# Two weight blocks by plain products instead of a seven-product scheme, in a fused attention, gated layer and expert layer kernel

## The chip, the cores and the metric

One core of one Trainium2 chip runs the whole program. The metric is the time of one execution on the device in microseconds (us). Shorter is better. The kernel before takes 825.68 us, the median of 3 runs (825.63 to 825.71).

## The reference

Three layers follow each other, in float32.

```python
# attention: 4 sequences, 8 heads, 576 positions, head size 64
scores = scale * q @ k.T ; scores + bias where 0 <= rel < 128, else -1e9
attn = softmax(scores) ; x = attn @ v          # 2304 tokens x 512
# gated layer, 512 -> 1536 -> 512
gate = 1 / (1 + exp(-(x @ w_gate))) ; val = x @ w_val
x = (gate * val) @ w_out
# expert layer: 8 experts, one per token by the largest cosine logit
h = maximum(x[mask] @ w1[e], 0) ; out[mask] = gate_w * (h @ w2[e])
```

The change touches the attention's last units and the products `x @ w_gate` and `x @ w_val`.

## The kernel before

**Attention** runs in 36 units (`unit_s`, `unit_n`, `unit_t`, `unit_b`). A unit is 256 query positions of two heads. TensorE (PE) makes its scores (24 small matmuls, L220, tile `s`), VectorE (DVE) adds the bias and takes the maximum in four "tails" (L231), ScalarE (ACT) takes the exponential (L234), DVE makes the reciprocal sums `rs` (L249, L250), GpSimd (POOL) scales the rows (L111), PE transposes them (L263, tile `t`), the transposes are copied to `tt` by ACT (L99) and DVE (L101), and PE multiplies them by v (L285, L291), again in `t`. The results are copied into `xf`, one tile per group of tokens ("chunk") and half of the 512 features. In a loop step i stand the transposes of unit i, the product with v of unit i-1 and the scores of unit i+3. A unit's scores take both buffers `s`, so they wait for the tails of the unit before.

**The gated layer's first products** go by 12 blocks of 128 columns of w_gate and w_val (index f). A float32 number is split into a high part and a rest (`split_x` for x, `split_w` for weights, each a cast on ACT, L99, and a 128x1024 subtraction on DVE, L115), and a product of two such pairs takes three matmuls (`product`, L403), so a piece of 256 features is six matmuls of 128x512. A raw block is loaded as two tiles `wr` (`load_w`), and made from 64-bit words by `conv_w` (one ACT operation and three on DVE, L125 to L128, for each half).

**The scheme.** Four chunks of 512 tokens form two pairs. For a pair, a block of weights and the x of two chunks are a 2x2 by 2x2 product, and `seven` makes it with seven products (`m1` to `m7`) instead of eight, from A11, A12, A22 and B11, B21, B22 as they are, and from sums of x, S1 to S4 (`sum_x`, one 128x1024 DVE operation each, L313, then split), and of weights, T1 to T4 (`sum_w`, four DVE operations L365 to L369, then split). `rg` and `rv` are the products of a chunk left over (12 matmuls of 128x256 each, L460).

The weights and their sums are also stored to device memory (`wf_d`, `tf_d`) and loaded again by `load_wt` for the second pair, where only the splits are left to do.

**The order** is written by hand. In units 0 to 19 the table `AT` (L515) lists for a loop step the work of the gated layer that stands behind it. From unit 20 on ("mixed units") a list `todo` holds the pieces, and beside each the work that is recorded with it; `run(n)` takes the next n. `STEPS` gives 3, 4 and then 5 pieces to a unit, 77 in all; the other pieces follow after the last unit. For all but the first blocks the work is that of `bulk(f)`, the preparation of block f+1. In units 10 to 19 only PE and POOL keep the written order, and a scheduler orders DVE and ACT; in the mixed units all four keep it. Every engine works its list in order, so an instruction that waits holds those behind it. All tiles of x and weights come from one pool of 33 buffers.

**The start.** `load_qk` and `load_v` bring a unit's q, k and v; `cst` brings the distance table `relm` and a tile `cs` with the identity for the transposes.

Of the kernel before, what the change touches and what calls it, by code (L numbers as in the profile page):

```python
# [27 lines left out]
P = 128  # L28
# [29 lines left out]
def attn_ffn_moe(ctx: ExitStack, tc: tile.TileContext, qkd, vd, wgv, w_out, emb, tau, w1, w2, cst, ids, out):  # L58
# [257 lines left out]
    def builds(pair):  # L316
        one, two = PAIRS[pair]

        def src(half, k):
            return xf[PAIRS[pair][half], k]  # L320

        return {
            "S1+": lambda: sum_x((pair, "S1"), src(1, 0), src(1, 1), ALU.add),
            "S3+": lambda: sum_x((pair, "S3"), src(1, 0), src(0, 0), ALU.subtract),
            "S2+": lambda: sum_x((pair, "S2"), xf[pair, "S1"], src(0, 0), ALU.subtract),
            "S4+": lambda: sum_x((pair, "S4"), src(0, 1), xf[pair, "S2"], ALU.subtract),
            "A11": lambda p="hl": split_x((pair, "A11"), src(0, 0), p),
            "A12": lambda p="hl": split_x((pair, "A12"), src(0, 1), p),
            "A22": lambda p="hl": split_x((pair, "A22"), src(1, 1), p),
            "S1": lambda p="hl": split_x((pair, "S1"), xf[pair, "S1"], p),  # L330
            "S2": lambda p="hl": split_x((pair, "S2"), xf[pair, "S2"], p),
            "S3": lambda p="hl": split_x((pair, "S3"), xf[pair, "S3"], p),
            "S4": lambda p="hl": split_x((pair, "S4"), xf[pair, "S4"], p),
        }
# [22 lines left out]

    def sum_w(f, part="01"):
        if f < KF:
# [46 lines left out]
    def gate_out(f, gate, val, t0, n):  # L406
        nc.vector.scalar_tensor_tensor(out=gate, in0=gate, scalar=1.0, in1=val, op0=ALU.add, op1=ALU.mult)
        nc.sync.dma_start(gT_d[f * P:(f + 1) * P, t0:t0 + n], gate)

    def seven(pair, f, banks, rest):  # L410
# [58 lines left out]

        def piece(mm, ev):  # L470
            def both():
                mm()
                ev()

            both.mm, both.ev = mm, ev
            return both

        out = {
# [14 lines left out]
    nc.sync.dma_start(relm[:, 0:4 * P], cst[:, 0:4 * P])  # L493
    load_qk(1)
    load_v(0)
    nc.sync.dma_start(cs, cst[:, 8 * P:])
    load_qk(2)
    load_v(1)
# [10 lines left out]
    def latest(*engines):  # L509
# [6 lines left out]
        5: [lambda: split_x("rest", xf[0, 0], "h")], 6: [lambda: split_x("rest", xf.pop((0, 0)), "l")],  # L516
        12: [bA["S1+"]], 13: [bA["A22"], lambda: load_w(0)], 14: [bA["S1"], lambda: conv_w(0, 0)],
        15: [lambda: conv_w(0, 1), lambda: load_w(1)], 16: [lambda: sum_w(0)],
        17: [bA["A11"], lambda: split_w(0, 0, 0)], 18: [bA["S3+"], lambda: split_w(0, 0, 1)],
        19: [bA["S3"], bA["S2+"], sA[0]["rg"]], 20: [bA["S2"], sA[0]["rv"]],  # L520
    }
    AB = {}
    with tc.manual_schedule(engines={ENG.PE, ENG.DVE, ENG.Activation, ENG.Pool}):
# [16 lines left out]
        unit_n(0)  # L540
        tails = unit_s(2, True)
        keep_warm(3)
        load_qk(6)
        unit_t(0)
        for t in tails:
            t()
        unit_n(1)
        for i in range(SPLIT):
# [45 lines left out]

    for f in range(KF):
        names, work = "m1 m2 m5 m6 rg m7 rv m4 m3", bulk(f)
        if f == 0:
            names = "m1 m5 m6 m7 m2 m4 m3"
            work = {
                0: [lambda: load_w(2), lambda: bA["A12"]("h")],  # L600
                1: [lambda: bA["A12"]("l"), lambda: conv_w(1, 0, "a")],
                2: [bA["S4+"], lambda: conv_w(1, 1, "a")],
                3: [lambda: bA["S4"]("h"), lambda: conv_w(1, 0, "b")],
                4: [lambda: bA["S4"]("l"), lambda: conv_w(1, 1, "b")],
                5: [lambda: split_w(0, 1, 0, "h"), lambda: sum_w(1)],
                6: [lambda: split_w(0, 1, 0, "l")],
            }
        elif f == 1:
            work[0].insert(0, lambda: split_w(0, 1, 1, "h"))
            work[1].insert(0, lambda: split_w(0, 1, 1, "l"))  # L610
        todo += [(sA[f][n], work.get(z, [])) for z, n in enumerate(names.split())]
# [86 lines left out]
    for t in ("A11", "A12", "S1+", "S1", "S2+"):  # L698
        run(1)
        bB[t]()  # L700
    split_w(1, 0, 0)
    run(2)
# [11 lines left out]
    for f in range(KF):  # L714
        s, t = sv[f], sv[f + 1] if f + 1 < KF else None
        s["m5"]()
        if f == 0:
            bB["A22"]()
            bB["S4+"]()
        split_w(1, f + 1, 0)  # L720
        s["m6"]()
# [522 lines left out]
```

## Time and profile before

| | |
|---|---|
| runs | 825.63 to 825.71 us, median 825.68 |
| the profiled execution | 824.9 us, of which the span from first to last instruction is 823.1 |
| PE, weight loads of PE, DVE, ACT, POOL busy | 97%, 80%, 67%, 54%, 21% of the span |
| granted TensorE clock | 0.996 of full speed, mean |

The share of a whole span hides stages. The kernel has one of attention alone (to about 47 us), one of attention with the preparation of the first block (to about 78), the mixed units, the second pair, and then the output product and the experts. The section with the rows has busy times by stretch. In a timeline a row's bracket is the idle time of that engine ahead of the instruction, and what ended it.

### The profile page before, as it was taken

Reading aid. Unit: us, or ns where it says so; the run is one execution under the profiler, and the core shown is the slowest. Engines: PE = TensorE matmul, PEld = TensorE weight load, DVE = VectorE, ACT = ScalarE, POOL = GpSimd, SP = SyncE. Lnnn points to the kernel's source line nnn. Section 1 sums busy time; section 2 is a strip of 40 time slices with the busy share of each in tenths; the row PEclk is TensorE's granted clock in tenths of the full one; section 3 lists DMA queues with packets and bytes.
Section 4 is the critical chain, followed back from the end, with each engine's and each line's share of the span. In section 5 each row is a group of like instructions: output and inputs, shape, how many; then the busy total and the mean of one; then the engine's idle time right before and its main releaser. Section 6 shows DMA issues by size and latency. Waiting matters only on the chain. (4 is left out here: it accounts for less than half of the span.)

```text
span 823.1 us, 15426 instructions
## 1 busy us (share of the span) xinstructions
PE 794.6 (97%) x5586; PEld 656.0 (80%) x5587; DVE 548.5 (67%) x1386; ACT 446.7 (54%) x942; POOL 174.6 (21%) x263
## 2 busy tenths in 40 slices
PE   8989799999999999999999999999999999999996
PEld 5767577888888788887777777778788988978885
DVE  6999887877788888788555544547645545545443
ACT  6888666766555666658455554435334434434331
POOL 5877332322100000000010000131322030230110
PEclk9999999999999999999999999999999999999999
DMA  8685655745555486668144555251565544453510
GB/s 268 191 257 177 223 194 194 238 156 179 174 186 208 158 276 230 220 227 257 56 128 145 144 141 156 82 138 55 183 228 171 190 170 141 151 203 118 175 69 19
DMA packets 67568, 141.45 MB, mean 172 GB/s; under 512 B 8440, under 2 KB 28664, under 8 KB 67490
## 3 DMA queue, kind: packets, MB, share of 16 engines
q1 hardware_dynamic: 63586, 130.32, 48.8%
q0 software_dynamic: 3904, 10.12, 3.7%
q8 instruction: 45, 0.74, 0.4%
q14 instruction: 33, 0.27, 0.1%
HBM read 104.14 MB, written 36.93 MB: 171 GB/s over the span
## 5 line engine op out<-in xcount | busy, mean ns | idle before, releaser
L806 PE MATMUL y<-wo,gh 128*128 128x512 f32 x432 | 139.3, 397 | 0.0
L986 PE MATMUL h<-xe,weh 128*128 128x256 f32 (+4 forms) x512 | 106.3, 301 | 0.9 <-DVE h L989 0.8
L111 POOL TENSOR_SCALAR p<-p,rs 128x192 f32<-128x192 f32 x140 | 80.3, 590 | 103.5 <-DVE rs L250 57.7
L1002 PE MATMUL z<-weh,h 128*128 128x512 f32 (+3 forms) x320 | 102.0, 396 | 0.0
L806 PEld LDWEIGHTS y<-wo,gh 128*128 128x128 f32 x432 | 79.9, 188 | 18.4 <-issue 3.3
L115 DVE TENSOR_TENSOR wel<-wer,weh 128x1024 fp32r<-128x1024 f32 x64 | 78.1, 1223 | 19.1 <-ACT weh L99 18.2
L986 PEld LDWEIGHTS h<-xe,weh 128*128 128x128 f32 x512 | 83.7, 189 | 3.3 <-DVE h L989 1.9
L806 PE MATMUL y<-wo,gl 128*128 128x512 f32 x216 | 84.9, 394 | 0.0
L988 ACT ACTIVATE h<-h 128x256 fp32r<-128x256 f32 (+4 forms) x64 | 26.6, 417 | 96.8 <-PE h L986 92.4
L234 ACT ACTIVATE p<-p,mx 128x192 f32<-128x192 f32 x144 | 64.0, 447 | 24.7 <-DVE mx L231 23.9
L986 PE MATMUL h<-xe,wel 128*128 128x256 f32 (+4 forms) x256 | 76.4, 300 | 0.2 <-DVE wel L115 0.2
L99 ACT CAST weh<-wer 128x1024 fp32r<-128x1024 f32 x64 | 66.2, 1048 | 7.0 <-DMA wer<-in_w 7.0
L1002 PEld LDWEIGHTS z<-weh,h 128*128 128x128 f32 (+3 forms) x320 | 56.7, 180 | 14.0
L1002 PE MATMUL z<-wel,h 128*128 128x512 f32 (+3 forms) x160 | 62.7, 392 | 0.0
L1007 POOL DMA_INDIRECT out<-y,cols x19 | 24.4, 1284 | 171.6 <-DVE y L1006 154.8
L989 DVE SCALAR_TENSOR_TENSOR h<-h,h 128x256 fp32r<-128x256 f32 (+4 forms) x64 | 29.6, 464 | 38.4 <-ACT h L988 35.5
L1006 DVE TENSOR_SCALAR y<-z,xg 128x512 f32<-128x512 f32 (+3 forms) x22 | 16.5, 749 | 56.0 <-PE z L1002 49.1
L900 POOL DMA_INDIRECT tab_d<-ids_sb,ai x18 | 18.3, 1015 | 158.7 <-DVE ai L897 136.5
L822 ACT ACTIVATE xr<-y 128x512 f32<-128x512 f32 x18 | 10.8, 598 | 73.4 <-PE y L806 66.3
L986 PEld LDWEIGHTS h<-xe,wel 128*128 128x128 f32 x256 | 48.4, 190 | 0.7 <-DVE wel L115 0.6
L806 PEld LDWEIGHTS y<-wo,gl 128*128 128x128 f32 x216 | 40.6, 188 | 8.0
L827 DVE COPY xT<-tl 128x512 f32<-128x512 f32 x18 | 12.4, 692 | 40.6 <-PE tl L826 40.6
(332 smaller groups left out, 1933.1 us busy)
## 6 DMA issues: line engine op xcount, KB each, us to landing
wer<-in_w SPq DMA_DIRECT2D x64, 512.0 KB, 4.3
gl<-gT_d SPq DMA_DIRECT2D x27, 512.0 KB, 5.6
wr<-in_wgv SPq DMA_DIRECT2D x24, 512.0 KB, 4.9
gT_d<-c SPq DMA_DIRECT2D x48, 256.0 KB, 2.0
qk<-in_qkd SPq DMA_DIRECT2D x36, 320.0 KB, 3.3
v<-in_vd SPq DMA_DIRECT2D x36, 192.0 KB, 4.0
wf_d<-wf SPq DMA_DIRECT2D x12, 512.0 KB, 2.9
tf_d<-tf SPq DMA_DIRECT2D x12, 512.0 KB, 3.4
```

Of the source, the lines that this page charges most:

```text
L99: nc.scalar.copy(o, i)
L111: nc.gpsimd.tensor_scalar(out=t, in0=t, scalar1=r, scalar2=0.0, op0=ALU.mult, op1=ALU.add)
L115: e.tensor_tensor(out=o, in0=i, in1=h.bitcast(F32), op=ALU.subtract)
L234: nc.scalar.activation(out=o, in_=o, func=AF.Exp, scale=-1.0, bias=mx[:, z:z + 1], accum_out=su[:, z:z + 1])
L806: nc.tensor.matmul(m, g[:, k % 4, u * P:(u + 1) * P], w[:, k % 3, :], start=(k == 0 and z == 0), stop=(k == KF - 1 and z == 2))
L900: nc.gpsimd.indirect_dma_start(out=tab_d, out_offset=IOA(ap=ai[:, u:u + 1], axis=0), in_=ids_sb[:, t:t + 1], in_offset=None)
L986: nc.tensor.matmul(m[:, :n], w[:, fs], x[:, k, :], start=(cnt == 0), stop=(cnt == 3 * KD - 1))
L988: nc.scalar.activation(out=hh, in_=m[:, :n], func=AF.Relu)
L989: nc.vector.scalar_tensor_tensor(out=hl, in0=m[:, :n], scalar=0.0, in1=hh.bitcast(F32), op0=ALU.max, op1=ALU.subtract)
L1002: nc.tensor.matmul(m[0:w, :], h, ww[:, ds], start=(cnt == 0), stop=(cnt == 3 * KE - 1))
L1006: nc.vector.tensor_scalar_mul(y[0:w, :], m[0:w, :], x[0:w, DM:DM + 1])
L1007: nc.gpsimd.indirect_dma_start(out=out, out_offset=IOA(ap=idx[0:w], axis=0), in_=y[0:w, :], in_offset=None, bounds_check=NT - 1, oob_is_er ...
```

## The change

Blocks 0 and 1 of the first pair are made by a new function `eight`, which takes eight plain products; they need no S and no T, but a split of A21. The blocks from 2 on keep the scheme. The S sums and their splits, which stood in `AT` and beside block 0, now stand beside the pieces of blocks 0 and 1. The T sums of blocks 0 and 1 are made at the start of the second pair, from the weights that are loaded again (`store=False`), so their two stores and two loads fall away. `rg` and `rv` of block 0 stand one step earlier. The list of pieces has 108 entries, where it had 106. At the start, q and k of the third unit are loaded third, v of the first unit after `cs`, and the third unit's tails are no longer put behind the first unit's transposes.

```diff
+NC = 2
...
+            "A21": lambda p="hl": split_x((pair, "A21"), src(1, 0), p),
...
-    def sum_w(f, part="01"):
+    def sum_w(f, part="01", store=True):
...
-                nc.sync.dma_start(tf_d[f * P:(f + 1) * P, :], flat(t))
+                if store:
+                    nc.sync.dma_start(tf_d[f * P:(f + 1) * P, :], flat(t))
...
-            for z, (d, src) in enumerate(((wf, wf_d), (tf, tf_d))):
+            for z, (d, src) in list(enumerate(((wf, wf_d), (tf, tf_d))))[:1 if f < NC else 2]:
...
+    def eight(pair, f):
+        st = {}
+
+        def mm(kind, chunk, half):
+            k = kind, chunk
+            if half == 0:
+                st[k] = pt("m", f"{kind}{pair}{chunk}_{f}", 3)
+            product(st[k], wq[pair, f, f"B{half + 1}{1 if kind == 'g' else 2}"], xs[pair, f"A{chunk}{half + 1}"], half == 0)
+
+        def ev(kind, chunk):
+            if kind == "g":
+                st["t", chunk] = row(f"th{pair}{chunk}_{f}")[:, 0:512]
+                nc.scalar.activation(out=st["t", chunk], in_=st["g", chunk], func=AF.Tanh, scale=0.5)
+            else:
+                gate_out(f, st["t", chunk], st["v", chunk], tok(PAIRS[pair][chunk - 1]), 512)
...
     load_qk(1)
+    load_qk(2)
+    nc.sync.dma_start(cs, cst[:, 8 * P:])
     load_v(0)
-    nc.sync.dma_start(cs, cst[:, 8 * P:])
-    load_qk(2)
...
-        12: [bA["S1+"]], 13: [bA["A22"], lambda: load_w(0)], 14: [bA["S1"], lambda: conv_w(0, 0)],
-        15: [lambda: conv_w(0, 1), lambda: load_w(1)], 16: [lambda: sum_w(0)],
-        17: [bA["A11"], lambda: split_w(0, 0, 0)], 18: [bA["S3+"], lambda: split_w(0, 0, 1)],
-        19: [bA["S3"], bA["S2+"], sA[0]["rg"]], 20: [bA["S2"], sA[0]["rv"]],
+        12: [bA["A21"]], 13: [bA["A22"], lambda: load_w(0)], 14: [lambda: conv_w(0, 0)],
+        15: [lambda: conv_w(0, 1), lambda: load_w(1)], 16: [lambda: split_w(0, 0, 0)],
+        17: [bA["A11"]], 18: [sA[0]["rg"], bA["S1+"]], 19: [sA[0]["rv"]], 20: [lambda: conv_w(1, 0)],
...
-        tails = unit_s(2, True)
+        unit_s(2)
         keep_warm(3)
         load_qk(6)
+        unit_n(1)
         unit_t(0)
-        for t in tails:
-            t()
-        unit_n(1)
...
+        (cA[0]["g2a"], [lambda: load_w(2), lambda: bA["A12"]("h")]),
+        (cA[0]["g2b"], [lambda: bA["A12"]("l"), lambda: conv_w(1, 1, "a")]),
+        (cA[0]["v2a"], [lambda: conv_w(1, 1, "b"), lambda: split_w(0, 1, 0, "h")]),
+        (cA[0]["v2b"], [lambda: split_w(0, 1, 0, "l"), lambda: bA["S1"]("h")]),
+        (cA[0]["g1a"], [lambda: bA["S1"]("l")]),
+        (cA[0]["g1b"], [bA["S3+"]]),
+        (cA[0]["v1a"], [bA["S2+"], lambda: bA["S3"]("h")]),
+        (cA[0]["v1b"], [lambda: bA["S3"]("l")]),
+        (sA[1]["rg"], [bA["S4+"], lambda: bA["S2"]("h")]),
+        (cA[1]["g2a"], [lambda: bA["S2"]("l"), lambda: conv_w(2, 0, "a"), lambda: load_w(3)]),
+        (cA[1]["g2b"], [lambda: conv_w(2, 0, "b"), lambda: conv_w(2, 1, "a")]),
+        (sA[1]["rv"], [lambda: conv_w(2, 1, "b"), lambda: split_w(0, 2, 0, "h")]),
+        (cA[1]["v2a"], [lambda: sum_w(2, "0")]),
+        (cA[1]["v2b"], [lambda: sum_w(2, "1"), lambda: bA["S4"]("h")]),
+        (cA[1]["g1a"], [lambda: split_w(0, 2, 0, "l")]),
+        (cA[1]["g1b"], [lambda: bA["S4"]("l"), lambda: split_w(0, 2, 1, "h")]),
+        (cA[1]["v1a"], [lambda: split_w(0, 2, 1, "l")]),
+        (cA[1]["v1b"], []),
...
+    sum_w(0, store=False)
     split_w(1, 0, 0)
...
+        if f + 1 < NC:
+            sum_w(f + 1, store=False)
         split_w(1, f + 1, 0)
```

On DVE at the start, ahead of unit 3's tails (`p0`, `p1`, `p2` are the rows of units 0 to 2, `tt0` the copies of unit 0's transposes), the order before is:

```order
L109 TENSOR_SCALAR p0_154<-p0_154,rs0_199 128x192 x2
L101 COPY tt0_0_229<-t0_0_228 128x384
L101 COPY tt0_1_235<-t0_1_234 128x384
L231 ISA p2_220,mx2_221<-s2_0_206,edge2_0_132 128x192
...
L249 TENSOR_SCALAR rs1_248<-su1_183 128x4
L250 RECIPROCAL rs1_248<-rs1_248 128x4
L109 TENSOR_SCALAR p1_181<-p1_181,rs1_248 128x192 x2
```

and with the change:

```order
L110 TENSOR_SCALAR p0_154<-p0_154,rs0_199 128x192 x2
L232 ISA p2_220,mx2_221<-s2_0_206,edge2_0_132 128x192
...
L250 TENSOR_SCALAR rs1_236<-su1_183 128x4
L251 RECIPROCAL rs1_236<-rs1_236 128x4
L110 TENSOR_SCALAR p1_181<-p1_181,rs1_236 128x192 x2
L102 COPY tt0_0_244<-t0_0_243 128x384
L102 COPY tt0_1_250<-t0_1_249 128x384
```

Unit 2's tails and the scaling of `p1` moved ahead of the copies of unit 0's transposes.

On DVE at steps 15 to 17, with the first block's preparation (`xl` is the rest of a split x, `wl00_0` the rest of block 0's weights, `tf0` its T sums, `tt15` and `tt17` copies of transposes), before:

```order
L115 TENSOR_TENSOR xl_(0, 'S1')_1215<-xq_(0, 'S1')_1076,xh_(0, 'S1')_1214 128x1024
L101 COPY xf2_0_1102<-t14_1_1155 128x128
L249 TENSOR_SCALAR rs17_1251<-su17_1203 128x4
L101 COPY tt15_1_1230<-t15_1_1229 128x384
...
L365 TENSOR_TENSOR tf0_1359<-wf0_1218 128x256
L366 TENSOR_TENSOR tf0_1359<-wf0_1218 128x256
L368 TENSOR_TENSOR tf0_1359<-wf0_1218,tf0_1359 128x256
L101 COPY tt17_1_1372<-t17_1_1371 128x384
L369 TENSOR_TENSOR tf0_1359<-wf0_1218,tf0_1359 128x256
```

and with the change:

```order
L102 COPY tt15_1_1228<-t15_1_1227 128x384
L102 COPY xf2_0_1104<-t14_1_1157 128x128
L250 TENSOR_SCALAR rs17_1249<-su17_1205 128x4
L251 RECIPROCAL rs17_1249<-rs17_1249 128x4
...
L116 TENSOR_TENSOR wl00_0_1358<-wf0_1216,wh00_0_1357 128x1024
L102 COPY tt17_1_1368<-t17_1_1367 128x384
L102 COPY xf2_2_1385<-t16_1_1298 128x128
```

The split of S1 and the four operations of the T sums are gone from here, and the split of block 0's weights, which stood behind A11's, has their place.

On DVE around the first mixed units, before, ahead of the first piece's need for S2 (`sg0_0` is the output of block 0's `rv`):

```order
L115 TENSOR_TENSOR xl_(0, 'S3')_1570<-xq_(0, 'S3')_1501,xh_(0, 'S3')_1569 128x1024
L313 TENSOR_TENSOR xq_(0, 'S2')_1573<-xq_(0, 'S1')_1076,xf2_0_1102 128x1024
L101 COPY xf2_2_1389<-t19_1_1513 128x128
L407 SCALAR_TENSOR_TENSOR sg0_0_1588<-sg0_0_1588,r_0_1575 128x256
L249 TENSOR_SCALAR rs22_1643<-su22_1558 128x4
L250 RECIPROCAL rs22_1643<-rs22_1643 128x4
L115 TENSOR_TENSOR xl_(0, 'S2')_1607<-xq_(0, 'S2')_1573,xh_(0, 'S2')_1606 128x1024
```

and with the change, where these sums stand now, beside the outputs `th02_0` and `th01_0` of block 0's `v2` and `v1`:

```order
L116 TENSOR_TENSOR wl00_1_1713<-wf1_1602,wh00_1_1712 128x1024
L410 SCALAR_TENSOR_TENSOR th02_0_1695<-th02_0_1695,v02_0_1701 128x512
L116 TENSOR_TENSOR xl_(0, 'S1')_1742<-xq_(0, 'S1')_1508,xh_(0, 'S1')_1741 128x1024
...
L314 TENSOR_TENSOR xq_(0, 'S2')_1814<-xq_(0, 'S1')_1508,xf2_0_1104 128x1024
...
L116 TENSOR_TENSOR xl_(0, 'S3')_1817<-xq_(0, 'S3')_1799,xh_(0, 'S3')_1816 128x1024
L410 SCALAR_TENSOR_TENSOR th01_0_1801<-th01_0_1801,v01_0_1807 128x512
L314 TENSOR_TENSOR xq_(0, 'S4')_1863<-xf2_2_1385,xq_(0, 'S2')_1814 128x1024
```

S1's and S3's splits and the sums S2 and S4 moved behind the split of block 1's weights and between the outputs of block 0.

## Rows read from the trace of the kernel before

**Rows 1.** The page's part 1: busy time of each engine, its share of the span.

```profile
PE 794.6 (97%) x5586; PEld 656.0 (80%) x5587; DVE 548.5 (67%) x1386; ACT 446.7 (54%) x942; POOL 174.6 (21%) x263
```

**Rows 2.** Busy time of each engine in five stretches, granted clock, DMA share, GB/s.

```profile
20.00:47.00 27.00, 25.61 (x538) 21.32 (x533) 24.15 (x127) 23.20 (x92) 22.20 (x56) 1.00 0.66 191
47.00:78.00 31.00, 26.20 (x430) 20.29 (x428) 29.55 (x112) 25.93 (x87) 22.26 (x41) 0.94 0.76 243
78.00:116.00 38.00, 32.59 (x321) 25.78 (x320) 31.90 (x77) 25.80 (x68) 15.99 (x22) 1.00 0.56 190
116.00:220.00 104.00, 101.70 (x941) 84.62 (x940) 81.71 (x205) 68.11 (x181) 28.17 (x46) 1.00 0.59 193
255.00:290.00 35.00, 34.44 (x167) 28.53 (x167) 31.25 (x35) 21.86 (x31) 0.00 (x0) 1.00 0.52 177
```

**Rows 3.** Timeline of DVE, first 14 us: start, us, instruction, idle before it.

```profile
7.19 0.41 DVE L795 CAST tri<-cs 128x128 bf16<-128x128 f32 x1 [0.52 <-DMA cs<-in_cst]
...
10.44 1.02 DVE L101 COPY tt<-t 128x384 f32<-128x384 f32 x2 [0.74 <-PE t L263]
```

**Rows 4.** Timeline of PE: the start, and units 18 to 20 to the first product.

```profile
12.11 1.39 PE L220 MATMUL s<-qk 64*64 64x128 f32 x24 [1.30 <-issue]
...
68.43 1.30 PE L220 MATMUL s<-qk 64*64 64x128 f32 x24
69.66 0.87 PE L263 MATMUL t<-cs,p 128*128 128x128 f32 x6
70.47 0.66 PE L285 MATMUL t<-tt,v 128*64 128x128 f32 x8
...
72.19 0.43 PE L220 MATMUL s<-qk 64*64 64x128 f32 x2
...
73.73 0.39 PE L460 MATMUL r<-xh_rest,wh 128*128 128x256 f32 x1
...
78.11 0.48 PE L403 MATMUL a<-xh_(0, 'A11')_1428,wh 128*128 128x512 f32 x1
```

**Rows 5.** Timeline of DVE, 55 to 72 us.

```profile
55.07 1.36 DVE L115 TENSOR_TENSOR xl_(0, 'S1')_1215<-xq_(0, 'S1')_1076,xh_(0, 'S1')_1214 128x1024 fp32r<-128x1024 f32 x1
...
63.57 0.56 DVE L365 TENSOR_TENSOR tf<-wf 128x256 f32<-128x256 f32 x1
64.05 0.41 DVE L366 TENSOR_TENSOR tf<-wf 128x256 f32<-128x256 f32 x1
...
67.11 1.37 DVE L115 TENSOR_TENSOR xl_(0, 'A11')_1429<-xf,xh_(0, 'A11')_1428 128x1024 fp32r<-128x1024 f32 x1
...
69.22 1.23 DVE L115 TENSOR_TENSOR wl<-wf,wh 128x1024 fp32r<-128x1024 f32 x1
...
71.60 1.36 DVE L313 TENSOR_TENSOR xq_(0, 'S3')_1501<-xf,xf 128x1024 f32<-128x1024 f32 x1
```

**Rows 6.** Timeline of PE, 86 to 142 us: the waits of blocks 0 and 1, and later.

```profile
86.09 0.50 PE L403 MATMUL a<-xh_(0, 'S3')_1569,wh 128*128 128x512 f32 x1 [1.09 <-ACT r L437]
...
95.62 0.50 PE L403 MATMUL a<-xh_(0, 'A11')_1428,wh 128*128 128x512 f32 x1 [1.04 <-ACT wh L99]
...
98.54 0.50 PE L403 MATMUL a<-xh_(0, 'A11')_1428,wl 128*128 128x512 f32 x1 [2.18 <-DVE wl L115]
...
108.86 0.50 PE L403 MATMUL a<-xh_(0, 'S3')_1569,wh 128*128 128x512 f32 x1 [1.08 <-ACT r L437]
...
116.36 0.39 PE L403 MATMUL a<-xh_(0, 'A11')_1428,wh 128*128 128x512 f32 x1
...
141.59 1.03 PE L285 MATMUL t<-tt,v 128*64 128x128 f32 x8 [0.77 <-ACT tt L99]
```

**Rows 7.** Timeline of PE: the first of six matmuls of two products in a row.

```profile
221.02 0.40 PE L403 MATMUL a<-xh_(0, 'A11')_1428,wh 128*128 128x512 f32 x1
...
222.40 0.39 PE L403 MATMUL b<-xh_(0, 'A12')_1661,wh 128*128 128x512 f32 x1
```

More of the change, by code (lines that the diff above doesn't have):

```diff
@@ L408, in gate_out, with piece, both @@
         nc.sync.dma_start(gT_d[f * P:(f + 1) * P, t0:t0 + n], gate)
+    def piece(mm, ev):
+        def both():
+            mm()
+            ev()
+        both.mm, both.ev = mm, ev
+        return both
+    def eight(pair, f):
[11 more added lines that the diff above has]
+                gate_out(f, st["t", chunk], st["v", chunk], tok(PAIRS[pair][chunk - 1]), 512)
+        out = {}
+        for kind in "gv":
+            for chunk in (1, 2):
+                out[f"{kind}{chunk}a"] = piece(lambda k=kind, c=chunk: mm(k, c, 0), lambda: None)
+                out[f"{kind}{chunk}b"] = piece(lambda k=kind, c=chunk: mm(k, c, 1), lambda k=kind, c=chunk: ev(k, c))
+        return out
     def seven(pair, f, banks, rest):
@@ L468, in rest_ev @@
                 gate_out(f, st["sg"][:, 0:256], m, tok(0), 256)
[L470 to L476, printed above, removed]
         out = {
@@ L516, in attn_ffn_moe @@
         5: [lambda: split_x("rest", xf[0, 0], "h")], 6: [lambda: split_x("rest", xf.pop((0, 0)), "l")],
-        12: [bA["S1+"]], 13: [bA["A22"], lambda: load_w(0)], 14: [bA["S1"], lambda: conv_w(0, 0)],
-        15: [lambda: conv_w(0, 1), lambda: load_w(1)], 16: [lambda: sum_w(0)],
-        17: [bA["A11"], lambda: split_w(0, 0, 0)], 18: [bA["S3+"], lambda: split_w(0, 0, 1)],
-        19: [bA["S3"], bA["S2+"], sA[0]["rg"]], 20: [bA["S2"], sA[0]["rv"]],
+        12: [bA["A21"]], 13: [bA["A22"], lambda: load_w(0)], 14: [lambda: conv_w(0, 0)],
+        15: [lambda: conv_w(0, 1), lambda: load_w(1)], 16: [lambda: split_w(0, 0, 0)],
+        17: [bA["A11"]], 18: [sA[0]["rg"], bA["S1+"]], 19: [sA[0]["rv"]], 20: [lambda: conv_w(1, 0)],
     }
+    cA = [eight(0, f) for f in range(NC)]
     AB = {}
@@ L593, in bulk @@
         }
-    for f in range(KF):
-        names, work = "m1 m2 m5 m6 rg m7 rv m4 m3", bulk(f)
[L597 to L610, printed above, removed]
+    todo += [(p, w) for p, w in [
+        (cA[0]["g2a"], [lambda: load_w(2), lambda: bA["A12"]("h")]),
[16 more added lines that the diff above has]
+        (cA[1]["v1b"], []),
+    ]]
+    for f in range(NC, KF):
+        names, work = "m1 m2 m5 m6 rg m7 rv m4 m3", bulk(f)
+        if f == NC:
+            work[0] = [lambda: load_w(4), lambda: conv_w(3, 0, "a")]
         todo += [(sA[f][n], work.get(z, [])) for z, n in enumerate(names.split())]
```

## The prediction

> **What bounds the kernel now.** I read the busy shares first. PE is busy 97% of the span [rows 1], so in most of the kernel only fewer matmuls would help, and this change adds some. The second view, busy time by stretch, tells where that is not so [rows 2]. From 116 to 220 us PE works 101.70 of 104. From 47 to 78 us it works 26.20 of 31, and there DVE is full: 29.55 of 31. From 78 to 116 us PE works 32.59 of 38, with DVE at 31.90. So PE loses 4.8 and 5.4 us in these two stretches, and about 2.3 in the next 104 us. The third view is the timeline of PE. From 78 to 116 us four waits make up all of the 5.4: 1.09 and 1.08 for an ACT copy that frees a bank, and 1.04 and 2.18 at the first product of block 1, for the high part and the rest of that block's weights [rows 6]. From 47 to 78 us the waits are short and many; there the timeline of DVE shows no gaps, only attention's tails with 128x1024 operations between them [rows 5].
>
> Behind 116 us PE is the bound, so whatever lets it get there earlier or later counts in full.
>
> **What is added to PE.** Two blocks take eight products instead of seven. Where PE runs without a wait, the first matmuls of two products in a row stand 1.38 us apart [rows 7]. Two products more: +2.76 us. The two entries more in the list of pieces are these products, nothing else. The plain products also spare block 0 and block 1 three ACT copies and three DVE additions each; these are beside PE's work, and I count them only as room.
>
> **Before the first product.** I follow DVE, since it is full there.
>
> At the start, DVE idles 0.74 us for unit 0's transposes and then copies them, with unit 2's tails behind [rows 3]; scores of unit 3 wait 1.30 us for those tails' buffers [rows 4]. With the tails ahead of the copies the 0.74 is filled. But `cs` now lands behind a 320 KB tile instead of a 192 KB one, and DVE already waits 0.52 us for it with unit 1's tails queued behind [rows 3]. Bounds: a loss as large as that wait, 0.5, and a gain of the whole 1.30. I take a gain of 0.4, nearer to the 0.74 that DVE can fill than to the wait of PE, because from there on DVE's next tails follow on without a gap.
>
> Up to the tails of unit 20, which end where the split of A11 begins at 67.11 [rows 5], DVE loses S1's split (1.36) and the four T operations (0.56 and 0.41, twice: 1.94); S1's sum and A21's split are one 128x1024 operation each and cancel. It gains, ahead of these tails, block 0's weight split (1.23), which stood behind them. Net 1.36 + 1.94 - 1.23 = 2.07. With the 0.4 of the start these tails end at 67.11 - 2.47 = 64.64, and then the scores of unit 21 can start.
>
> From there on PE has more to do than DVE. Its path to the first product: scores of unit 21 (0.9, an estimate under the 1.30 that they took at 68.43, since the stretch's granted clock of 0.94 is a mean over a slow part and a full one), transposes of 19 (0.81, from 69.66 to 70.47), unit 18 with v (1.2, from 70.47 to 72.19 less a wait), and then scores of 22, `rg`, unit 19 with v, `rv` and transposes of 20, which took from 72.19 to 78.11, or 5.92 [rows 2, 4]. That is 8.83, and the first product starts at 73.47 instead of 78.11: **-4.64 us**, the start included. Bounds: if DVE's freed time came back only as its sum after the start, 2.07; if PE recovered all that it idles before 78 us in this stretch, 4.8 + 1.3 = 6.1. `rg` one step earlier costs nothing, since PE has room in front of it.
>
> **From the first product to block 2.** Before, block 2 starts at 116.36 [rows 6]. The four waits sum to 5.39. I expect them to go. The two for the ACT copy belong to m6 and m7, which use one bank; `eight` has no such pair, and its three banks let a product start while two others are read out. The two for block 1's weights came since their split was queued on DVE behind block 0's S and T work. Now it stands ahead of S1's split, and block 1's first product is the tenth piece where it was the eighth.
>
> What is late next is block 2's split. DVE was busy 31.90 us between block 0's first product and block 2's [rows 2]. It loses the T sums of block 1 (1.94), their split (1.23) and six additions of outputs there, and gets S1's and S3's splits and S3's sum (1.36 or 1.37 each [rows 5]); some 32 us or less. PE has 32.59 + 2.76 = 35.35 for the same pieces and units, and DVE can begin while PE is still on its 5.92 us from unit 22's scores to the first product: 41 together. DVE idled 38 - 31.90 = 6.1 us in that stretch before; 32 + 6.1 fits under 41. So I leave no wait there, but little room. One wait I do add: the mixed units' transposes are both copied by ACT, and unit 20's copies stand behind four exponentials while only one piece covers them. The nearest row is such a wait later, 0.77 [rows 6]; bounds 0 and 2.18, the longest wait of this stretch. Sum of this part: -5.39 + 2.76 + 0.77 = **-1.86 us**.
>
> **Behind it.** Blocks 2 to 8 keep their pieces and work. The waits of 116 to 220 us (2.3) fall where a block's start meets a unit's; the two pieces more shift this, I count no change.
>
> At the start of the second pair DVE gets two more sums, eight 128x256 operations of 0.41 to 0.56: +3.9 us at most. In 255 to 290 us it is busy 31.25 of 35, so 3.75 is free, and PE idles 0.56 there [rows 2]. Bounds: 0, and 3.9 if none of the free time lies where it helps. I take +0.2: the scheduler put other operations into DVE's gaps. The two stores and two loads of 512 KB that fall away hide beside PE now, and are worth nothing. SP's queue gets shorter; the weight loads in it come no later.
>
> Sum: -4.64 - 1.86 + 0.2 = -6.3 us. The profiled execution takes 824.9 and becomes 818.6. It stands 0.8 under the median, so in the terms of the runs 825.7 - 6.3 = **819.4 us**.
>
> The Trainium skill (Perfetto Trace Analysis, Identifying the Most-Contended Engine) says to take the engine of highest occupancy as the most contended one and to work on that one first, but for TensorE to go by the busy share of its weight loads, not of its matmuls. By the first half the page's 97% speaks against any added matmul; by the second PE has room, and the trace agrees that weight loads fall to 20.29 of 31 us (65%) from 47 to 78 us, against 84.62 of 104 (81%) later [rows 2].
>
> **The rivals.**
>
> *DVE was not what paced 47 to 78 us.* The scaling on POOL and the exponentials on ACT are in each unit's chain too, with 22.26 and 25.93 of 31 busy [rows 2]. If one of them takes over, only about half of the 4.64 comes: 825.7 - 2.3 - 1.86 + 0.2 = 821.7; with part of block 2's waits coming back as well, up to 824. For it: PE's waits there name many engines. Against it: neither has DVE's share.
>
> *More comes back.* PE also recovers its stretched matmuls, loses the half-speed clock (0.94 mean from 47 to 78 us, full in the other stretches [rows 2]) and shows no new wait: the full 6.1 and none of the 0.77 give 825.7 - 6.1 - 2.63 = 817.0, and 815 if some of the later 2.3 goes too.
>
> *Slower: the wait moves to block 2.* Place: block 2's first product, which needs its split behind the S sums. Price: DVE works its 32 us in order, held up by PE's scores and outputs. It decides from the point where DVE idles over 41 - 32 = 9 us in that stretch, and the result is slower than before only from 9 + 6.3, some 15 us. At 18 us of idling the new wait is 9, and 819.4 + 9 = 828.4. Before, it idled 6.1 there, which is the evidence against.
>
> *The added products are a plain loss.* If PE is the bound everywhere, the time saved before block 2 would be met by other waits, and only the two products are left: 825.7 + 2.76 = 828.4. The four named waits, 5.39 us on PE itself, speak against it. This is also what the first half of the skill's rule, read over the whole span, would give.
>
> *Nothing moves*, gains and added products cancel: within 0.2%, or 1.65 us, which is about what a measurement of this kernel can tell from no change.
>
> **How the numbers follow.** The forecast, from 817.5 to 821, has 0.52. The half gain (821 to 824) has 0.20, the larger one (814.5 to 817.5) 0.17, no change 0.04, block 2's wait 0.04, the plain loss 0.03. All of the first three are faster by over 1.65 us: 0.89; same 0.04; slower 0.07. For the range I cut the larger gain at 816.0 and the half gain at 822.8, which leaves out about 0.2.
>
> **What would show it.** In the changed kernel's profile: the first product of block 0 at 73 to 74 us; DVE still nearly full from 47 to 65 us, and PE with hardly a wait from there on; no wait of over 1 us between the first product and block 2's, which starts at about 110 us; 14 plus 2 products of 1.38 us there; PE's idle time between 255 and 290 us under 1 us. I am wrong if the first product comes later than 76 us, if block 2's first product waits for `wl` or `wh`, or if the second pair starts with a wait of microseconds.

## The result and the profile after

The changed kernel takes **817.40 us** (median of 6 runs, 816.95 to 817.86) against 825.69 us of the kernel before (6 runs, five from 825.53 to 825.99 and one of 828.26), a ratio of 0.9897, interval 0.9887 to 0.9908: 8.3 us less, where 6.3 were forecast. That lies in the stated range of 816.0 to 822.8, but 0.1 us below the part from 817.5 to 821 that was held likeliest. The profiled execution takes 817.27 us, its span is 815.4.

The page's busy shares, of the changed kernel:

```profile
PE 794.9 (97%) x5598; PEld 657.9 (81%) x5599; DVE 542.5 (67%) x1379; ACT 443.4 (54%) x935; POOL 170.8 (21%) x263
```

The same five stretches as in [rows 2] (PE, PEld, DVE, ACT, POOL, granted clock, DMA share, GB/s):

```profile
20.00:47.00 27.00, 25.32 (x528) 20.93 (x525) 24.62 (x123) 23.41 (x91) 21.76 (x55) 1.00 0.64 188
47.00:78.00 31.00, 27.33 (x488) 22.02 (x487) 26.52 (x112) 25.89 (x93) 24.19 (x46) 1.00 0.82 266
78.00:116.00 38.00, 38.00 (x350) 31.30 (x350) 31.25 (x78) 26.18 (x71) 12.87 (x22) 1.00 0.61 200
116.00:220.00 104.00, 102.01 (x921) 84.81 (x920) 82.23 (x199) 67.34 (x174) 25.41 (x40) 1.00 0.54 181
255.00:290.00 35.00, 35.00 (x167) 29.19 (x166) 29.89 (x42) 21.72 (x31) 0.00 (x0) 1.00 0.56 193
```

PE's share has not moved by a point. What moved is 78 to 116 us: PE went from 32.59 busy to all 38.00, and its weight loads from 25.78 to 31.30 [rows 2]. From 47 to 78 us DVE is no longer full (26.52 of 31 for 29.55), yet PE still loses 3.67. The timeline of PE shows where, and the landmarks used below: block 0's first product (74.25), block 2's (109.56), and the second pair's first (265.51).

```profile
56.88 0.52 PE L264 MATMUL t<-cs,p 128*128 128x128 f32 x3 [1.08 <-ACT xf L100]
...
64.69 0.85 PE L264 MATMUL t<-cs,p 128*128 128x128 f32 x6 [0.96 <-ACT xf L100]
...
74.25 0.48 PE L406 MATMUL g<-xh_(0, 'A21')_1076,wh 128*128 128x512 f32 x1
...
109.56 0.39 PE L406 MATMUL a<-xh_(0, 'A11')_1424,wh 128*128 128x512 f32 x1
...
119.96 0.50 PE L406 MATMUL a<-xh_(0, 'S3')_1816,wh 128*128 128x512 f32 x1 [0.83 <-ACT r L471]
...
265.51 0.39 PE L406 MATMUL a<-xh_(1, 'A11')_3807,wh 128*128 128x512 f32 x1
...
554.22 0.49 PE L1021 MATMUL h<-xe,weh 128*128 128x256 f32 x2
```

Two landmarks of the kernel before, from its timeline of PE: the second pair's first product and the first matmul of the expert layer.

```profile
272.82 0.39 PE L403 MATMUL a<-xh_(1, 'A11')_3827,wh 128*128 128x512 f32 x1
...
562.47 0.49 PE L986 MATMUL h<-xe,weh 128*128 128x256 f32 x2
```

So the forecast's terms came out as follows (us, changed less before; block 0's first product of before is in [rows 4]):

| stretch | forecast | measured |
|---|---|---|
| start to block 0's first product | -4.64 | 74.25 - 78.11 = -3.86 |
| from there to the second pair | -1.86 | 191.26 - 194.71 = -3.45 |
| second pair to the expert layer | +0.2 | 288.71 - 289.65 = -0.94 |
| expert layer to the end of the span | 0 | 261.18 - 260.63 = +0.55 |
| sum | -6.3 | -7.70 |

The two profiled executions differ by 7.7 us and the medians by 8.3, since the one before stood 0.8 under its median and the changed one 0.1.

**What holds 47 to 65 us now.** ACT's timeline of the changed kernel, then DVE's:

```profile
55.92 0.66 ACT L120 ACTIVATE wf<-wr 128x512 f32<-128x512 f32 x1 [0.63 <-DMA wr<-in_wgv]
56.48 0.25 ACT L100 COPY xf<-t 128x128 f32<-128x128 f32 x1
```

```profile
56.61 0.43 DVE L126 TENSOR_SCALAR wf<-wf 128x512 int32<-128x512 int32 x1 [0.91 <-ACT wf L120]
...
65.91 1.22 DVE L116 TENSOR_TENSOR xl_(0, 'A11')_1425<-xf,xh_(0, 'A11')_1424 128x1024 fp32r<-128x1024 f32 x1
```

ACT's first conversion of block 0's raw weights waits 0.63 for their DMA. The copy of attention's output `xf` stands behind it on ACT, and PE waits 1.08 for that copy at 56.88; DVE waits 0.91 for the conversion. The Trainium skill (PSUM — Partial Sum Buffer, Engine vs sequencer instructions) says that the queue of ScalarE is strict FIFO; the trace agrees: ACT idles 0.63 ahead of the conversion though the matmuls that the copy reads ended at 54.66, and the 0.25 us copy starts only when the conversion ends.

### The profile page after: what moved, and what is told of

It reads as the page before. It is cut to its first block, busy times and chain, and to the rows that moved or that the text cites. A ratio compares the mean times of both kernels' runs of the same rounds, so it can differ in the third digit from the quotient of the medians.

```text
span 815.4 us, 15417 instructions
## 1 busy us (share of the span) xinstructions
PE 794.9 (97%) x5598; PEld 657.9 (81%) x5599; DVE 542.5 (67%) x1379; ACT 443.4 (54%) x935; POOL 170.8 (21%) x263
## 5 line engine op out<-in xcount | busy, mean ns | idle before, releaser
L112 POOL TENSOR_SCALAR p<-p,rs 128x192 f32<-128x192 f32 x140 | 76.3, 561 | 99.3 <-DVE rs L251 50.9
```

Of the source, the lines that this page charges most:

```text
L112: nc.gpsimd.tensor_scalar(out=t, in0=t, scalar1=r, scalar2=0.0, op0=ALU.mult, op1=ALU.add)
```

## The experiments

Times are medians beside the kernel before on the same chip; with a median for the changed kernel of 817.4 and 817.8 in its two sets of runs, differences under one us are read from landmarks in the trace.

### The start alone

On the kernel before:

```diff
-    load_v(0)
-    nc.sync.dma_start(cs, cst[:, 8 * P:])
     load_qk(2)
+    nc.sync.dma_start(cs, cst[:, 8 * P:])
+    load_v(0)
...
-        tails = unit_s(2, True)
+        unit_s(2)
...
-        unit_t(0)
-        for t in tails:
-            t()
         unit_n(1)
+        unit_t(0)
```

> The kernel before with the part of the change at the start alone (load order, and unit 2's tails ahead of the copies for unit 0). My theory: DVE paces up to 68 us, so the whole gain of the start arrives: about -0.4 us, 825.3, with the tails of unit 3 about 0.4 us earlier. Rival (the start makes most of what the first stage gained): -2 us or more, 823.7 or less. Rival (the start is absorbed by later waits): no difference, 825.7.

Measured: 824.10, ratio 0.9981 (0.9971 to 0.9991), so 0.7 to 2.4 us less. In the trace the scores that waited 1.30 at 12.11 [rows 4] start at 10.77 with no wait, and block 0's first product moved by 1.53:

```profile
10.77 0.89 PE L220 MATMUL s<-qk 64*64 64x128 f32 x24
...
76.58 0.48 PE L403 MATMUL a<-xh_(0, 'A11')_1428,wh 128*128 128x512 f32 x1
```

My theory of 0.4 us lies outside the interval. In this execution the start alone was worth the 1.30 that stood as its upper bound. It isn't worth that in every one: a product with v near 30 us, used below as the landmark of the start, comes 1.25 earlier here (29.84 for 31.09) and only 0.43 earlier in the first profile of the changed kernel, in which DVE waits 0.70 for `cs`:

```profile
31.09 0.66 PE L285 MATMUL t<-tt,v 128*64 128x128 f32 x8 [0.75 <-ACT tt L99]
```

```profile
30.66 0.66 PE L286 MATMUL t<-tt,v 128*64 128x128 f32 x8 [0.75 <-ACT tt L100]
```

### One and three plain blocks

NC = 1, with block 1's T sums and their split back in the first stage, and NC = 3, with block 2 as a third plain block and its T sums in the second pair. With one, the list also has another order from there on. The core of the two edits to the list of pieces:

```diff
-        (cA[0]["v2b"], [lambda: split_w(0, 1, 0, "l"), lambda: bA["S1"]("h")]),
+        (cA[0]["v2b"], [lambda: sum_w(1, "0"), lambda: bA["S1"]("h")]),
...
-        (cA[1]["g2a"], [lambda: bA["S2"]("l"), lambda: conv_w(2, 0, "a"), lambda: load_w(3)]),
+        (sA[1]["m1"], [lambda: bA["S2"]("l"), lambda: bA["S3"]("h")]),
```

```diff
-        (cA[1]["v2a"], [lambda: sum_w(2, "0")]),
+        (cA[1]["v2a"], []),
...
+    for p, w in zip([cA[2]["g2a"], cA[2]["g2b"], sA[2]["rg"], cA[2]["v2a"], cA[2]["v2b"], sA[2]["rv"], cA[2]["g1a"],
+                     cA[2]["g1b"], cA[2]["v1a"], cA[2]["v1b"]], range(10)):
+        todo.append((p, bulk(2).get(w, [])))
```

> The changed kernel with one plain block instead of two: block 1 goes by seven products again, with its T sums (1.94 us of DVE) and their split (1.23 to 1.37) made during block 0; all of the work of the two blocks is the same apart from that. My theory: one product less is -1.38; but DVE and ACT get 3.3 and 1.0 us more in a stretch where DVE is 31.25 us busy of 38, and block 1 has the pair m6 and m7 on one bank again: waits of 2 to 4 us come back before block 2, so 818.0 to 820.0, point 819.0. Rival (the added products are a plain loss, and the gain came from the first stage and the order of the splits alone): -1.38, 816.0. Rival (all of the second stage's gain needs both plain blocks): the four waits of before but one, +2.94, 820.3.

> The changed kernel with a third plain block: block 2 takes eight products, its T sums go to the second pair. My theory: the waits before block 2 are gone already, so there is only block 2's own 0.83 us wait for the copy of m6 to take away, and +1.38 to pay, with 0.97 us more for DVE at the second pair's start, hidden or nearly: +0.3 to +1.6, point 818.2. Rival (each plain block brings its share of the gain): -3 us or more, 814.4 or less. Rival (a product is hidden beside other waits and costs nothing): -0.8, 816.6.

Measured: one plain block 822.31 (ratio 0.9953, 0.9940 to 0.9965), three 820.37 (0.9939, 0.9926 to 0.9952): both slower than two, and the first above the 818 to 820 that I gave it (its profiled execution, the fastest of five, took 820.14). From block 0's first product to the second pair, which is untouched by what the start does in a run, one block takes 193.63 and three take 192.66, against 191.26. The waits of PE in the kernel with one:

```profile
102.19 0.50 PE L406 MATMUL a<-xh_(0, 'S3')_1867,wh 128*128 128x512 f32 x1 [1.10 <-ACT r L471]
...
123.74 0.50 PE L406 MATMUL a<-xh_(0, 'S3')_1867,wh 128*128 128x512 f32 x1 [2.76 <-ACT r L471]
```

With four shorter ones (0.29, 0.37, and two further on), PE waits 6.06 in this stretch, 1.95 in the changed kernel: +4.11 for -1.38 gives +2.73, and the landmarks show +2.37. Against the kernel before the sum closes less well: waits of 1.62 less and one product more give -0.24, the landmarks show -1.08, and the difference stays open. The rival that added products are a plain loss falls: taking one away, with this order of the list, made the kernel slower. With three blocks the waits sum to 1.93, so none was left to remove, and 192.66 - 191.26 = 1.40 is the bare price of a product, 1.38 [rows 7]. I had expected 0.83 back from block 2's wait; it only moved to block 3 (0.82). The second pair, where the third block's sums stand now and where I had expected them hidden, takes 290.05 from its first product to the expert layer, +1.34. It has a new wait of 0.68, for an ACT copy; that the sums cause it is not shown by itself.

### Block 0's T sums made early again

```diff
-            for z, (d, src) in list(enumerate(((wf, wf_d), (tf, tf_d))))[:1 if f < NC else 2]:
+            for z, (d, src) in list(enumerate(((wf, wf_d), (tf, tf_d))))[:1 if f == 1 else 2]:
...
-        15: [lambda: conv_w(0, 1), lambda: load_w(1)], 16: [lambda: split_w(0, 0, 0)],
+        15: [lambda: conv_w(0, 1), lambda: load_w(1)], 16: [lambda: sum_w(0), lambda: tf.pop(0), lambda: split_w(0, 0, 0)],
...
-    sum_w(0, store=False)
     split_w(1, 0, 0)
```

> The changed kernel with the four T sums of block 0 made early again, ahead of that block's weight split, stored, and loaded for the second pair as before. It undoes one part that is DVE's alone, 1.94 us. My theory: DVE was what paced 47 to 68 us and has about 1.2 to 2 us of gaps there now, since ACT has taken over; so some 0.5 to 1.5 us of the 1.94 come back as a later first product, and DVE is full again there: 817.9 to 818.9, point 818.4. Rival (ACT or POOL paced that stretch all along, DVE's relief is worth nothing): first product at the same time, 817.4, or a little under, since the second pair has 0.97 us less for DVE. Rival (DVE still paces): the full 1.94, 819.3.

Measured: 821.14 (0.9941, 0.9928 to 0.9954), more than any theory gave. Its profiled execution and a second one of the changed kernel (below) agree to 0.04 us up to 57 us:

```profile
57.02 0.52 PE L264 MATMUL t<-cs,p 128*128 128x128 f32 x3 [1.90 <-ACT xf L100]
...
76.07 0.48 PE L406 MATMUL g<-xh_(0, 'A21')_1076,wh 128*128 128x512 f32 x1
...
273.68 0.50 PE L406 MATMUL a<-xh_(1, 'A11')_3815,wh 128*128 128x512 f32 x1 [0.39 <-ACT wh L100]
```

and the changed kernel:

```profile
56.98 0.87 PE L264 MATMUL t<-cs,p 128*128 128x128 f32 x3 [1.90 <-ACT xf L100]
...
74.39 0.48 PE L406 MATMUL g<-xh_(0, 'A21')_1076,wh 128*128 128x512 f32 x1
```

The first product comes 1.68 later. That is about all that the four sums take from DVE's queue: the 1.94 of the forecast and of the expectation is a sum of durations, and each of these records overlaps the next by about 0.08. From the start of one to the start of the next, in the kernel before, they hold DVE for 0.48, 0.34, 0.48 and 0.33, together 1.63 (the first two are in [rows 5]):

```profile
64.39 0.56 DVE L368 TENSOR_TENSOR tf<-wf,tf 128x256 f32<-128x256 f32 x1
64.87 0.55 DVE L101 COPY tt<-t 128x384 f32<-128x384 f32 x1
65.34 0.41 DVE L369 TENSOR_TENSOR tf<-wf,tf 128x256 f32<-128x256 f32 x1
65.67 0.28 DVE L101 COPY xf<-t 128x128 f32<-128x128 f32 x1
```

So behind 57 us DVE does pace this stretch; the idle time it has in 47 to 68 us is all ahead of that, while it waits for ACT and ACT for the weights. At the second pair a wait is back that the change had removed (0.39), and the stretch to the expert layer is 0.85 longer than in the changed kernel, though the sums that the changed kernel makes there cost DVE four operations of 0.42 us, some 1.35 from start to start (I had expected 0.97). In this kernel as in the one before, ACT's split of block 1's weights stands behind a tanh (`c`, L468) that waits for DVE; with the sums on the spot the scheduler puts it ahead. ACT's timeline here, then that of the changed kernel's first profile:

```profile
272.05 0.63 ACT L468 ACTIVATE c<-c 128x512 f32<-128x512 f32 x1 [2.22 <-DVE c L467]
272.59 1.03 ACT L100 CAST wh<-wt 128x1024 fp32r<-128x1024 f32 x1
```

```profile
267.56 1.05 ACT L100 CAST wh<-wt 128x1024 fp32r<-128x1024 f32 x1
269.69 0.63 ACT L468 ACTIVATE c<-c 128x512 f32<-128x512 f32 x1 [1.08 <-DVE c L467]
```

The two profiles differ by 3.38 in span. Of what is left, 0.41 lies between the first product and the second pair and 0.45 behind the start of the expert layer; the latter differs as much between two executions of the changed kernel (261.18 and 260.57).

### The changed kernel again, the loads apart, the copies on DVE

```diff
-        12: [bA["A21"]], 13: [bA["A22"], lambda: load_w(0)], 14: [lambda: conv_w(0, 0)],
-        15: [lambda: conv_w(0, 1), lambda: load_w(1)], 16: [lambda: split_w(0, 0, 0)],
-        17: [bA["A11"]], 18: [sA[0]["rg"], bA["S1+"]], 19: [sA[0]["rv"]], 20: [lambda: conv_w(1, 0)],
+        11: [lambda: load_w(0)], 12: [bA["A21"]], 13: [bA["A22"]], 14: [lambda: conv_w(0, 0)],
+        15: [lambda: conv_w(0, 1)], 16: [lambda: split_w(0, 0, 0)],
+        17: [bA["A11"], lambda: load_w(1)], 18: [sA[0]["rg"], bA["S1+"]], 19: [sA[0]["rv"]], 20: [lambda: conv_w(1, 0)],
```

```diff
-                hi_copy("v" if i < 11 or j and i < NA else "a", x[:, j * P:(j + 1) * P], os[j])
+                hi_copy("v" if i < NA else "a", x[:, j * P:(j + 1) * P], os[j])
```

> The changed kernel, unedited, beside the next three on one chip. Theory (the first stage has an unsteady part: ACT's first conversion waits for block 0's raw weights, which land about 56 us after the start whatever the engines did before, 0.63 us here and 1.15 to 1.75 in three runs of kernels with the same first 50 us): 817.4 to 819, with the first product of block 0 between 74.2 and 75.5 and the wait of ACT as what differs. Rival (that stage is steady and the edits alone moved it): 817.4 and 74.25 again.

> The changed kernel with the raw weights of block 0 loaded two units earlier and those of block 1 two units later, so that the 1 MB each are no longer in flight together. Theory (the landing of block 0's weights holds ACT, ACT holds the copy that PE waits for at 57 us): ACT's wait of 0.63 to 1.75 and PE's of 1.08 to 2.19 go, no half-speed stretch; DVE has its gap filled and is the pacer again, so 0.7 to 1.5 us of it arrive: 816.0 to 816.8 against 817.4 to 818. Rival (DVE paces, its gap there is harmless): within 0.3 us of the changed kernel. Rival (the loads collide with qk and v instead): PE waits for qk or v, slower by 1 or more.

> The changed kernel with attention's output copies of units 11 to 19 all on DVE, nine of them moved off ACT (0.25 us each there, 0.28 on DVE). The same wait of PE is attacked from the other side: the copy no longer stands behind ACT's conversion. Theory (the copy behind ACT's wait for the weights is what holds PE at 57 us): PE's waits for xf by ACT, 2.6 us in three, go, but DVE has 2.5 us more to do in a stretch where it was idle some 2 us: first product 0.3 to 1.5 us earlier, 816.2 to 817.1 against 817.4. Rival (DVE is at its limit there already): 1 to 2.5 us later, 818.4 to 820.

> The loads apart and the copies on DVE together. Theory (both remove the same wait): no better than the better one of the two, and since DVE has no gap left, worse than the loads apart alone by up to 1.5: 816.5 to 818. Rival (they remove different waits): the two gains add, 815 or less.

Measured: the changed kernel 817.84 (0.9908, 0.9893 to 0.9924), loads apart 817.62, copies on DVE 817.43, both 816.68 (0.9890, 0.9873 to 0.9906); no two can be told apart by time. The trace of the changed kernel bears out the theory of the landing: its landmark near 30 us comes 0.73 us earlier than in the first trace (29.93 for 30.66), and ACT then waits longer, for weights that land at nearly the same time (its conversion starts at 55.92 and at 56.03), so the first product is at 74.39 for 74.25.

```profile
56.03 0.66 ACT L120 ACTIVATE wf<-wr 128x512 f32<-128x512 f32 x1 [1.46 <-DMA wr<-in_wgv]
```

With the loads apart ACT waits for no weights and from 47 to 78 us no stretch has a lower clock, as expected, but the first product stays at 74.29, and the 816.0 to 816.8 of my theory was missed. Part of that is the start, whose landmark comes at 30.84 in this execution, 0.91 later than in the second one of the changed kernel. Part is a side effect: the scheduler moved A21's split on DVE ahead of copies that PE needs:

```profile
45.00 0.89 PE L264 MATMUL t<-cs,p 128*128 128x128 f32 x6 [1.23 <-DVE xf L102]
...
57.46 0.52 PE L264 MATMUL t<-cs,p 128*128 128x128 f32 x3 [1.31 <-ACT xf L100]
```

With the copies on DVE my theory failed: PE waits 2.04 at 58.73 instead, for scores of the next unit, and the first product comes at 75.51. The profile names no releaser there; DVE idles 1.55 just then ahead of its own conversion step, which needs ACT's, with a unit's tails queued behind. Late weights hold up the chain on DVE as well as on ACT. With both edits the first product comes at 75.01; no gains add up there.

### One cast later, one load earlier

```diff
-    nc.vector.tensor_copy(tri, tri_f)
+    tc.keep_in_program_order(nc.vector.tensor_copy(tri, tri_f))
```

```diff
-        12: [bA["A21"]], 13: [bA["A22"], lambda: load_w(0)], 14: [lambda: conv_w(0, 0)],
+        12: [bA["A21"], lambda: load_w(0)], 13: [bA["A22"]], 14: [lambda: conv_w(0, 0)],
```

> The changed kernel with one DVE instruction moved: the cast of the triangle constant, which the scheduler puts at the head of DVE's queue, ahead of unit 1's tails, and which is needed only at routing, stands where routing's other constants are made. Theory (this cast alone makes DVE wait for `cs`, 0.17 to 1.55 us in the runs so far, and is why the start differs from run to run; but behind it the landing of block 0's raw weights at 56 us absorbs what is gained): the transposes of unit 0 and the copies behind them come without that wait, the landmark near 30 us at 29.7 to 29.9 in place of 29.9 to 31.0, the first product still between 74.0 and 74.5, ACT's wait for the weights 1.4 or more; 817.4, within 0.5 us of the changed kernel. Rival (the start arrives whole): 816.5 to 817.0. Rival (the transposes need `cs` at the same time anyway): nothing moves, not even the landmark.

> The changed kernel with the raw weights of block 0 loaded one unit earlier and nothing else edited; the scheduler then puts both conversions of ACT ahead of a unit's exponentials. Theory (the landing of these weights is what sets 55 to 58 us): ACT's and DVE's wait for it go, DVE is the pacer throughout, first product at 73.0 to 74.2, 816.2 to 817.3. Rival (the unit chain of scores, tails, exponentials, scaling and transposes sets the pace, as with the loads apart, where the wait went and the product did not move): first product at 74.2 or later, 817.4 to 818.2.

> Both of these together. Theory (once the weights land earlier the start's gain is no longer absorbed): first product at 72.5 to 73.5, 815.8 to 816.5, more than the sum of the two alone. Rival (the chain of a unit sets the pace behind 47 us): the sum of the two alone or less, 817 or more.

Measured: the cast 817.35 (0.9893, 0.9876 to 0.9909), the load **815.73** (0.9871, 0.9855 to 0.9888), both **815.29** (0.9867, 0.9850 to 0.9883). The cast alone did what was expected: DVE no longer waits for `cs`, the landmark near 30 us is at 29.45, ACT waits 1.44 for the weights, and the first product is at 74.42. But the cast is not the whole reason why the start differs: in the three profiled executions with the later cast the landmark is at 29.45, 30.54 and 29.64, and in the second of these DVE waits 1.00 and 0.73 for scores, ahead of the tails of units 0 and 1, where the first has 0.57 and no wait over 0.15. (The wait for `cs` was 0 to 1.55 in the runs so far, not 0.17 to 1.55.) The load, recorded one loop step earlier, is issued 10 us earlier, at 39.71 and 42.28 in place of 49.97; ACT's first conversion then starts at 52.13 without a wait. From SyncE's timeline of the changed kernel, then of the one with the load alone:

```profile
49.97 0.89 SPq L347 DMA_DIRECT2D wr<-in_wgv  x2
```

```profile
39.71 0.42 SPq L347 DMA_DIRECT2D wr<-in_wgv  x1
```

Both kernels with the earlier load came out below their stated ranges. The two edits together beat both kernels: 1.33% (1.17 to 1.50) less than the one before, some 11 us, where the change has 1.03% (0.92 to 1.13); the cast's share in that can't be told from nothing. DVE works from 50 to 68 us without a gap. DVE's timeline and PE's:

```profile
64.77 1.21 DVE L116 TENSOR_TENSOR xl_(0, 'A11')_1425<-xf,xh_(0, 'A11')_1424 128x1024 fp32r<-128x1024 f32 x1
```

```profile
30.54 0.66 PE L286 MATMUL t<-tt,v 128*64 128x128 f32 x8 [0.75 <-ACT tt L100]
...
63.73 0.84 PE L264 MATMUL t<-cs,p 128*128 128x128 f32 x6 [1.13 <-POOL p L112]
...
73.30 0.48 PE L406 MATMUL g<-xh_(0, 'A21')_1076,wh 128*128 128x512 f32 x1
```

These are the numbers that the forecast had for the changed kernel: tails of unit 20 at 64.64, first product at 73.47. Counted from the landmark, the tails end 34.23 behind it, for 67.11 - 31.09 = 36.02 in the kernel before. That is 1.79 less: what moved off DVE ahead of them, counted from start to start (S1's split 1.28, from 55.07 to 56.35; the T sums 1.63; less block 0's weight split, 1.14, from 69.22 to 70.36), is 1.77. Whether the two gains do more than add can't be told at this precision.

The last run puts block 0's T sums early on top of that:

> The kernel with the earlier load and the later cast, and on top of it the four T sums of block 0 made early, stored and loaded for the second pair, as in the run that did this to the changed kernel alone. Theory (with the weights there in time DVE has no gap from 50 to 65 us, so its work counts in full): the tails of unit 20 end 1.9 us later than 64.77, the first product comes at 75.0 to 75.4 instead of 73.30 (1.5 later still if the clock falls to half speed in the stretch), and the second pair starts 0.5 to 0.9 us slower, since ACT's high part of block 1's weights is late again: 817.5 to 818.3 against 815.3. Rival (ACT, POOL or the chain of a unit paces): the first product within 0.6 us of 73.30, 815.3 to 816.4.

Measured: 819.73 (0.9939, 0.9926 to 0.9953), above the range that I gave. In the profiled execution, the fastest of five (817.03), the tails of unit 20 end 35.87 us behind the landmark near 30 us, against 34.23 without the sums: 1.64, for the 1.63 that they hold DVE. The first product, at 73.81, is 1.41 later by the same measure; the 75.0 to 75.4 that I gave for it left out that the start differs by 0.9 between the two executions.

```profile
29.64 0.66 PE L286 MATMUL t<-tt,v 128*64 128x128 f32 x8 [0.74 <-ACT tt L100]
...
73.81 0.48 PE L406 MATMUL g<-xh_(0, 'A21')_1076,wh 128*128 128x512 f32 x1
```

```profile
65.51 1.25 DVE L116 TENSOR_TENSOR xl_(0, 'A11')_1431<-xf,xh_(0, 'A11')_1430 128x1024 fp32r<-128x1024 f32 x1
```

DVE's work there counts in full up to the tails, and the rival falls. The other four runs took 819.55 to 820.97; that their mean granted clock was 0.994 or 0.995, for 0.999, fits a half-speed stretch, but they left no trace.

## Why the prediction was right, and which terms were off

**Before the first product (-4.64, came as -3.86).** The path was right: DVE paced it, as the two runs with the T sums made early show. The terms, with the landmark near 30 us as the end of the start:

| term | forecast | measured |
|---|---|---|
| the start | -0.4 | 30.66 - 31.09 = -0.43 |
| DVE up to the tails of unit 20 | -2.07 | 35.25 - 36.02 = -0.77 |
| PE behind these tails | -2.17 | 8.34 - 11.00 = -2.66 |

"DVE loses 2.07" was mis-sized twice. It sums durations that overlap, where 1.77 comes out from start to start. And it was summed as if DVE stayed full; the tails ended at 65.91, not 64.64, since DVE idled for conversions that waited for the weights' DMA. I had written that the weight loads "come no later", which is true, but the engines had come earlier. PE's own work behind the tails took 8.34 where 8.83 was counted, which made up for part of it. That the start came out as forecast is luck: it was 1.25 in the run of the start alone, and 1.16 in the second profile of the changed kernel, where the 0.73 more did not reach the first product.

**From the first product to the second pair (-1.86, came as -3.45).** The four waits went, all 5.39; a product costs its 1.38 where no wait is left, as the third block shows. The wait for unit 20's copies, +0.77, did not come. The waits behind 116 us fell from 2.30 to 1.95. That makes -5.39 + 2.76 - 0.35 = -2.98; for the 0.47 that is left I have an estimate only: behind a matmul that has waited the next one starts 0.33 us after it, elsewhere 0.23, and PE has five waits fewer (eight before, three after), which makes 0.5.

```profile
86.42 0.39 PE L403 MATMUL a<-xl_(0, 'S3')_1570,wh 128*128 128x512 f32 x1
86.65 0.39 PE L403 MATMUL a<-xh_(0, 'S3')_1569,wl 128*128 128x512 f32 x1
```

These two follow the wait at 86.09 [rows 6].

**The second pair (+0.2, came as -0.94).** The sign was wrong: the two waits at its start, 0.56 together, disappeared, where I had asked only whether DVE had room. That the order of ACT's queue did it is read from the traces, not tried by itself; in both runs with the T sums made early a wait for ACT's `wh` is back (0.39 and 0.40). The 0.55 us that the expert layer took more is not the change's: in the second profile of the changed kernel it takes 260.57, for 260.63 before.

**The rivals.** More comes back than forecast, as in the larger-gain case (817.0), but by other terms: not from the stage before the first product. That another engine paced 47 to 78 us falls by the T sums made early: what they hold DVE for comes back as later tails of unit 20 (1.64 for 1.63). The plain loss is refuted by one plain block against two; block 2's split was not late, as its first product at 109.56 has no wait. The first half of the rule on the most contended engine in the Trainium skill (Perfetto Trace Analysis, Identifying the Most-Contended Engine) would have advised against the change; PE's 97% before and after it says nothing, and the weight loads' share from 78 to 116 us, 68% before and 82% after, does.

## What to carry to other kernels

Read an added product against the named waits of its own stretch: two blocks removed 5.39 us of waits for 2.76 of products and won, a third had no wait left to remove and cost its 1.38 and more. When a stage bound by a full engine is shortened, look for what arrives at a fixed time (here a load) and have it issued earlier, or the gain stops there. Count an engine's work from start to start of its records, not by their durations: 1.63 and 1.94 us for the same four operations here. Look at what a scheduler puts at the head of an in-order queue: here one cast that nothing needs for hundreds of microseconds, though moving it alone changed no time that these runs can tell.

## What the hardware showed that I had not expected

The half-speed clock comes and goes between executions with nearly the same waits. This is the stretch from 63.4 to 66.6 us of the kernel with the earlier load alone, then of the one with the later cast too:

```profile
63.40:66.60 3.20, 3.20 (x45) 2.54 (x47) 2.77 (x10) 2.88 (x11) 2.95 (x6) 0.50 0.34 110
```

```profile
63.40:66.60 3.20, 2.88 (x57) 2.50 (x58) 3.20 (x16) 3.20 (x13) 3.03 (x6) 1.00 0.62 236
```

The first is at 0.50 of full speed, the level of 1.2 GHz, the second at 2.4 GHz. In both PE had waited 1.26 at 56 us, then 0.16 or 0.17, then 1.13 at 63, for the same tiles; the first had one more wait, at 52.38 (0.54, for 0.15 in the second). The last run has all of them (0.54, 1.27, 0.16, and 1.30 at 63.01) and stays at 1.00. From the last of these waits to the first product it is 74.22 - 63.08 = 11.14 in the first and 73.30 - 63.73 = 9.57 in the second: the half-speed stretch cost 1.57 us. The same six transposes take 1.33 us in the one and 0.84 in the other:

```profile
63.08 1.33 PE L264 MATMUL t<-cs,p 128*128 128x128 f32 x6 [1.13 <-POOL p L112]
```

The Trainium skill (TensorE: Matmul & The Clock Gate, What's actually happening) says that the gate is closed by default and that activity opens it; what these traces add is that PE's waits in a profile do not tell in which of two such executions the clock falls.
